# PSUM handed out by single banks, and score pieces issued two by two, in an attention and MLP kernel

## The chip, the core and the metric

The kernel runs on one core of one Trainium2 chip. The metric is the device time of one execution in microseconds (us). Five engines work side by side, each through its own queue in order: TensorE (PE in the profile; its weight loads stand apart as PEld), VectorE (DVE), ScalarE (ACT), GpSimd (POOL) and SyncE (SP, which here only issues transfers). They meet through semaphores: an instruction may wait until another engine's count has reached a number. Matmul results go to PSUM, which has eight banks; a bank holds 512 float32 values per partition.

## The reference

Causal attention over 8 batches, 8 heads, 576 tokens and 64 features, with 16 "beacon" keys and values ahead of the sequence that every token sees; then an MLP with a squared ReLU over the 8 x 576 = 4608 tokens of 512 features:

```
k_all = concat([beacon_k, k]);  v_all = concat([beacon_v, v])
scores = q @ k_all.T / 8;       scores[causal] = -1e9
a = exp(scores - max); a /= sum(a)
x = (a @ v_all) laid out as [4608, 512]
h = x @ w_in                    # [4608, 2048]
out = (max(h, 0) ** 2) @ w_out  # [4608, 512]
```

## The kernel before, in words

**The attention.** The work goes by batch (8) and head pair (4), so 32 pairs. q and k are brought into a transposed form: for batches 0 to 2 on TensorE (line 405, with copies out of PSUM at 280 and 282), later by transposing transfers on SP (line 359). A pair's **scores** are matmuls with 64 rows, the two heads side by side in the two halves of the array (line 506). They come in *pieces*: four for a whole pair, 992, 928, 832 and 576 elements over both heads (batch 0 is split into two phases, with pieces of its own). A piece fills a two-bank tile of PSUM, ScalarE takes its exponential into SBUF (line 520), VectorE masks the diagonal (lines 530 and 534), TensorE multiplies with the values (line 550, with a column of ones that gives the row sums), VectorE normalizes (lines 565 and 566). The result is transposed into `xT`, on TensorE for batches 0 and 1 (line 614), by SP's transfers later (line 597).

**The MLP.** It goes by nine chunks of 512 tokens. For each chunk there are eight *units* (`emit_s1`, line 678): a unit makes two of the sixteen 128-wide slices of the hidden layer, eight matmuls of 512 columns into the two banks of one PSUM tile. One ReLU of 1024 elements empties the tile, on ScalarE (line 694) or VectorE (line 696), and VectorE squares (line 703). The second product (`emit_s2`, line 718) has two PSUM tiles per chunk, each with two token tiles of 128, 32 matmuls in all into each; ScalarE copies each tile out at once, 1024 elements (line 280), but for the last of the kernel, which is copied in two halves, and SP stores it (lines 750 and 752). Chunk 0 has its units in two parts (tokens 0 to 239 and 240 to 511).

**PSUM.** `ps` is four tiles `[128, 2, 512]` in float32, two banks each. Scores, value products, transposes and MLP units all take whole tiles from this one pool.

**The order.** A planner in the kernel's source (`Order.run`) decides it on the host: every operation has an engine (or two to choose from), an assumed duration, a priority, dependencies, and what it takes from a pool and gives back. The planner steps through time, starts on each free engine the ready operation of lowest priority number, and so fixes each engine's order of instructions and the PSUM tile of every operation. `limits` bounds how many tiles a class may hold (scores 2, value products 2, MLP 2, transposes 1). A `gate` holds the scores of a pair back until the MLP has made enough progress. The instructions are then emitted in that order, each engine's queue runs in order on the chip, and the framework puts in the semaphore waits between them from the tiles that they read and write.

Of the kernel before, what the change touches and what calls it, by code (L numbers as in the profile page):

```python
# [10 lines left out]
BF16 = mybir.dt.bfloat16  # L11
# [5 lines left out]
class Op:  # L17
# [4 lines left out]
                 "sync", "insts")  # L22

    def __init__(self, name, engs, dur, emit, prio=0.0, deps=(), take=None, give=None,
                 gate=None, dma=0.0, pe_time=0.0, behind=(), sync=()):
        self.name = name
        self.engs = engs if isinstance(engs, (tuple, list)) else (engs,)
        self.dur = dur
        self.emit = emit
        self.prio = prio  # L30
        self.sync = list(sync)
        self.need = list(deps) + self.sync
        self.users = []
        self.take = take
        self.give = give
        self.gate = gate
        self.held = None
        self.dma = dma
        self.pe_time = pe_time
        self.behind = list(behind)  # L40
        self.followers = []


class Order:
# [3 lines left out]
    LAT = {"PE": 0.2, "ACT": 0.2, "DVE": 0.15, "POOL": 0.25, "SP": 0.1, "-": 0.0}  # L48

    def __init__(self, pools, limits):  # L50
        self.pools = {k: list(v) for k, v in pools.items()}
        self.limits = dict(limits)
        self.inuse = {k: 0 for k in limits}
        self.ops = []
        self.progress = 0.0
# [7 lines left out]
    def run(self):  # L63
# [23 lines left out]
        now = 0.0  # L87
        while events:
            now = events[0][0]
            while events and events[0][0] <= now + 1e-9:  # L90
# [6 lines left out]
                elif kind == "give":  # L97
                    pool, cls, idx = op.give.held
                    self.pools[pool].append(idx)
                    if cls in self.inuse:  # L100
                        self.inuse[cls] -= 1
            again = True
            while again:
                again = False
                for e in engines:
# [3 lines left out]
                    fallback = None  # L109
                    for op in avail[e]:  # L110
                        if any(free[x] <= now + 1e-9 for x in op.engs[:op.engs.index(e)]):
                            continue
                        if op.take:
                            pool, cls = op.take
                            if not self.pools[pool]:
                                continue
                            if cls in self.limits and self.inuse[cls] >= self.limits[cls]:
                                continue
# [20 lines left out]
                    if op.take:  # L139
                        pool, cls = op.take  # L140
                        op.held = (pool, cls, self.pools[pool].pop(0))
                        if cls in self.inuse:
                            self.inuse[cls] += 1
                    dur = op.dur[e] if isinstance(op.dur, dict) else op.dur
                    end = now + dur
# [31 lines left out]
def kernel(  # L177
# [65 lines left out]

    def wait_for(later, first):
# [4 lines left out]
        pools={"ps": range(4), "stg": range(NSTG), "pt": range(NPT)},  # L249
        limits={"strip": 2, "av": 2, "mlp": 2, "tp": 1},  # L250
# [60 lines left out]
    def add_load(b, x, c, prio, behind=[], sync=[]):  # L311
# [10 lines left out]
        def emit_load(e):  # L322
            st = stg[ld.held[2]]
            insts = []
            if lo:
# [6 lines left out]
                 prio=prio, take=("stg", "stg"), dma=1.1 * rows / 128, behind=load_chain[-1:] + behind, sync=sync)  # L332
        load_chain.append(ld)

        def emit_cast(e):
            st = stg[ld.held[2]]
# [40 lines left out]
    def add_strided(b, prio):  # L377
# [17 lines left out]
        for pr in range(HP):  # L395
# [3 lines left out]
            def emit_tp(e, pr=pr, h=h, box=box):  # L399
                pp = ps[box["t"].held[2]].bitcast(BF16)  # L400
                nc.tensor.transpose(pp[:, 1, 0:Nb], bks[b % 2][:, h, :], ident[0:Nb, 0:Nb])
                for half, at, t in ((1, Nb, ks), (0, 0, qs)):
                    for u in range(NS):
# [5 lines left out]
            tp = add(f"tp{b}.{pr}", "PE", 0.8 if b else 1.3, emit_tp, prio=100.0 * (HP * b + pr) - 190,  # L409
                     deps=[bk, loads[pr, "k"], loads[pr, "q"], ident_op] + busy, take=("ps", "tp"))  # L410
            box["t"] = tp

            def emit_k(e, pr=pr, box=box):
                pp = ps[box["t"].held[2]].bitcast(BF16)
# [4 lines left out]
            def emit_q(e, pr=pr, box=box):  # L419
                pp = ps[box["t"].held[2]].bitcast(BF16)  # L420
# [3 lines left out]
            ek = add(f"ek{b}.{pr}", "DVE", 0.9, emit_k, prio=-200.0, deps=[tp])  # L424
            eq = add(f"eq{b}.{pr}", ("DVE", "ACT"), 0.75, emit_q, prio=-199.0, deps=[tp])
# [50 lines left out]
    def add_pair(b, pr):  # L476
# [12 lines left out]
        take_pt = add(f"pt{p}", "-", 0.0, None, prio=100.0 * p, deps=qk_deps, take=("pt", "pt"), gate=gate)  # L489
# [4 lines left out]
    def add_phase(b, pr, p, n, ph, take_pt, qk_deps, gate):  # L494
        base = 100.0 * p + 1000.0 * n
        exps = []
        for i, (mms, off, width) in enumerate(ph.pieces):
            cols = sum(max(96, t1 - t0) for _, t0, t1, _ in mms)
            box = {}

            def emit_qk(e, mms=mms, box=box):
                st = ps[box["qk"].held[2]]
                for c, t0, t1, at in mms:
                    for hj in range(2):
                        hp = slice(64 * hj, 64 * hj + 64)
                        nc.tensor.matmul(  # L506
                            st[:, hj, at:at + t1 - t0],
                            kT[b % 2][hp, pr, 128 * c:128 * c + 128],
                            qT[b % 2][hp, pr, t0:t1],
                            start=True, stop=True,  # L510
                        )

            qk = add(f"qk{p}.{n}.{i}", "PE", 0.05 + cols / 2400.0, emit_qk, prio=base + i,
                     deps=qk_deps + [take_pt], take=("ps", "strip"), gate=gate)
            box["qk"] = qk
            qk_ops[p].append(qk)

            def emit_exp(e, off=off, width=width, box=box):
                st = ps[box["qk"].held[2]]
                nc.scalar.activation(pt[take_pt.held[2]][:, :, off:off + width], st[:, :, 0:width],  # L520
                                     AF.Exp, bias=0.0, scale=scale)

            exps.append(add(f"exp{p}.{n}.{i}", "ACT", 0.18 + 2 * width / 1200.0, emit_exp, prio=base + i,
                            deps=[qk], give=qk))

        def emit_mask(e):
            P = pt[take_pt.held[2]]
# [9 lines left out]
        mask = add(f"mask{p}.{n}", "DVE", 0.15 + 0.14 * ph.diag[3] + (0.25 if ph.last else 0.0), emit_mask,  # L537
# [3 lines left out]
        def emit_av(e):  # L541
            P = pt[take_pt.held[2]]
            a = ps[av.held[2]]
            for hj in range(2):
                h = 2 * pr + hj
                for t in tl:
# [10 lines left out]
        av = add(f"av{p}.{n}", "PE", 0.07 + 0.064 * sum(t + 1 for t in tl), emit_av, prio=base - 150,  # L557
                 deps=[mask] + [cast[b, "v", c] for c in range(tl[-1] + 1)] + av_ops[p], take=("ps", "av"),
# [3 lines left out]
        def emit_norm(e):  # L562
            a = ps[av.held[2]][:, :, 0:nt * (D + 1)].rearrange("p h (t d) -> p h t d", d=D + 1)
# [12 lines left out]
        norm_ops[p, n] = add(f"norm{p}.{n}", "DVE", 0.4 + 0.133 * nt, emit_norm, prio=base - 150, deps=deps, give=av)  # L576
# [27 lines left out]
    def add_xt_pe(b):  # L604
        for k, ph in enumerate(phases(b)):
            for pr in range(HP):
# [3 lines left out]
                def emit_tp(e, pr=pr, box=box, ph=ph):  # L610
                    pp = ps[box["t"].held[2]].bitcast(BF16)
                    for t in ph.tiles:
                        n = t_rows(t)
                        nc.tensor.transpose(pp[:, 0, t_start(t):t_start(t) + n],
# [3 lines left out]
                         deps=[norm_ops[HP * b + pr, k]], take=("ps", "tp"))  # L618
                box["t"] = tp

                def emit_ev(e, pr=pr, box=box, lo=lo, hi=hi):
                    pp = ps[box["t"].held[2]].bitcast(BF16)
                    at = (b * S) % RING
                    copy_on(e, xT[:, pr, at + lo:at + hi], pp[:, 0, lo:hi])

                o = add(f"xte{b}.{k}.{pr}", ("ACT", "DVE"),
                        {"ACT": 0.2 + (hi - lo) / 1200.0, "DVE": 0.12 + (hi - lo) / 960.0}, emit_ev, prio=-110.0,
# [25 lines left out]
    def add_chunk(j):  # L653
# [11 lines left out]
        for f in range(NFT // 2):  # L665
            sqs = []
            for n, (lo_, hi_) in enumerate(parts):
                spans = [(lo_, wrap), (wrap, hi_)] if lo_ < wrap < hi_ else [(lo_, hi_)]
                N = hi_ - lo_
                box = {}  # L670

                def emit_s1(e, f=f, spans=spans, box=box):
                    h = ps[box["s1"].held[2]]
                    for u in range(2):
                        ft = 2 * f + u
                        for lo, hi in spans:
                            for mc in range(NMC):
                                nc.tensor.matmul(h[:, u, lo - spans[0][0]:hi - spans[0][0]],  # L678
# [4 lines left out]
                s1 = add(f"s1.{j}.{f}.{n}", "PE", 1.73 * N / TCH, emit_s1, prio=base + f + 0.5 * n,  # L683
                         deps=feeds_of(lo_, hi_) + [w_ops["in", f // 2]]
                         + [s2_ops[j - 2, u] for u in range(2) if j >= 2],
                         take=("ps", "mlp"), pe_time=1.73 * N / TCH)
                box["s1"] = s1
                s1_ops[lo_, hi_].append(s1)

                def emit_relu(e, f=f, lo=lo_ - t0, hi=hi_ - t0, box=box):  # L690
                    h = ps[box["s1"].held[2]][:, :, 0:hi - lo]
                    dst = G[:, 2 * f:2 * f + 2, lo:hi]
                    if e == "ACT":
                        nc.scalar.activation(dst, h, AF.Relu, bias=0.0, scale=1.0)  # L694
                    else:
                        nc.vector.tensor_scalar(out=dst, in0=h, scalar1=0.0, scalar2=None, op0=ALU.max)  # L696

                rl = add(f"relu{j}.{f}.{n}", ("ACT", "DVE"), {"ACT": 0.2 + N / 600.0, "DVE": 0.15 + N / 480.0},
                         emit_relu, prio=-20.0, deps=[s1], give=s1)
# [5 lines left out]
                sqs.append(add(f"sq{j}.{f}.{n}", "DVE", 0.1 + 0.6 * N / TCH, emit_sq, prio=-10.0, deps=[rl]))  # L705
            sq.append(sqs)
        prevs = {}
        if j == 0:
            order2 = [(u, [(ts, 4 * qd, 4 * qd + 4) for ts in range(2)], [qd]) for qd in range(4) for u in range(2)]
        else:  # L710
            order2 = [(u, [(ts, 8 * half, 8 * half + 8)], [2 * half, 2 * half + 1])
# [122 lines left out]
```

## Time and profile before

| | |
|---|---|
| time, median of 3 runs | 355.47 us (355.32 to 355.49) |
| span of the profiled execution, first to last instruction | 353.2 us |
| matmuls of the MLP's first product, line 678 (records) | 689 |
| matmuls of the MLP's second product, line 718 (records) | 554 |
| score matmuls, line 506 | 400 in 81 uninterrupted runs |
| exponentials, line 520 | 128, 105.3 us of ScalarE |
| ReLUs | 65 on ScalarE (61.8 us), 15 on VectorE (15.8 us) |
| output copies, ScalarE | 19, 18.3 us |

The profile comes from one execution; its own time is its span plus what lies around it, and the median of the runs is 2.3 us above the span. Its views: busy time per engine, also in 40 slices of the span with the clock that TensorE was granted; the chain of work that ended last, followed back from the end; groups of instructions by source line and shape, with count, busy time, mean duration in ns, and the idle time before them with what ended it; the list of waits (engine and line, what it waited for, us in total, times, longest); the timeline. In a row such as `PE L678 MATMUL ps<-xT,w_in 128*128 128x512 bf16 x8` the operation writes `ps` and reads `xT` and `w_in`, on 128 rows and 128 columns of the array, with 512 moving columns, eight times. A matmul's record runs on past the moment at which the next can start, so matmul durations overlap; what counts for the stream is from start to start. Some matmul records are missing.

### The profile page before, as it was taken

Reading aid. Unit: us, or ns where it says so; the run is one execution under the profiler, and the core shown is the slowest. Engines: PE = TensorE matmul, PEld = TensorE weight load, DVE = VectorE, ACT = ScalarE, POOL = GpSimd, SP = SyncE. Lnnn points to the kernel's source line nnn. Section 1 sums busy time; section 2 is a strip of 40 time slices with the busy share of each in tenths; the row PEclk is TensorE's granted clock in tenths of the full one; section 3 lists DMA queues with packets and bytes.
Section 4 is the critical chain, followed back from the end, with each engine's and each line's share of the span. In section 5 each row is a group of like instructions: output and inputs, shape, how many; then the busy total and the mean of one; then the engine's idle time right before and its main releaser. Section 6 shows DMA issues by size and latency. Waiting matters only on the chain.

```text
span 353.2 us, 7173 instructions
## 1 busy us (share of the span) xinstructions
PE 334.7 (95%) x2943; PEld 178.6 (51%) x2980; DVE 148.9 (42%) x287; ACT 193.4 (55%) x233; POOL 85.5 (24%) x132
## 2 busy tenths in 40 slices
PE   3789999999999989999999999999999999999994
PEld 2459665554545444444446874445454444444441
DVE  5576674349714455146622753247132302301300
ACT  2686786287555764665745663676634405505602
POOL 7273721209215504133501651000000000000000
PEclk9999999999999999999999999999999999999999
DMA  7999999965969999699989999440013103003003
GB/s 101 183 160 204 223 206 211 201 169 118 206 116 236 223 221 191 138 224 222 251 137 202 248 213 209 115 118 11 0 61 69 59 0 121 0 0 121 0 0 119
DMA packets 137008, 49.49 MB, mean 140 GB/s; under 512 B 123344, under 2 KB 132048, under 8 KB 136976
## 3 DMA queue, kind: packets, MB, share of 16 engines
q1 hardware_dynamic: 127472, 40.09, 53.4%
q0 software_dynamic: 9504, 8.95, 15.7%
q8 instruction: 23, 0.38, 0.5%
q14 instruction: 9, 0.07, 0.1%
HBM read 37.22 MB, written 9.44 MB: 132 GB/s over the span
## 4 chain that ended last, share of the span: by engine, by line
PE 74%; DMA 12%; SPq 5%; ACT 4%; DVE 2%; issue 2%; POOL 1%; ACTq 0%; DVEq 0%; POOLq 0%
PE ps L678 32%; PE ps L718 27%; PE ps L550 7%; PE ps L506 6%; DMA stg<-in_k_dram 4%; DMA stg<-in_v_dram 4%; SPq L597 3%; ACT pt L520 2%; DMA kT<-qk_area 2%; DMA stg<-in_q_dram 1%; SPq L327 1%; DVE kT L282 1%; DMA qk_area<-in_q_dram 1%; PE ps L405 1%; ACT qT L280 1%
## 5 line engine op out<-in xcount | busy, mean ns | idle before, releaser
L678 PE MATMUL ps<-xT,w_in 128*128 128x512 bf16 (+3 forms) x689 | 131.9, 340 | 1.6 <-ACT qT L280 0.6
L718 PE MATMUL ps<-w_out,g 128*128 128x512 bf16 x554 | 129.5, 380 | 1.4 <-issue 0.5
L520 ACT ACTIVATE pt<-ps 128x832 bf16<-128x832 f32 (+4 forms) x128 | 105.3, 865 | 40.7 <-PE ps L506 40.2
L678 PEld LDWEIGHTS <-w_in 128*128 128x128 bf16 x704 | 66.0, 98 | 57.6 <-issue 6.0
L694 ACT ACTIVATE g<-ps 128x1024 bf16<-128x1024 f32 (+2 forms) x65 | 61.8, 951 | 54.0 <-PE ps L678 53.8
L718 PEld LDWEIGHTS <-g 128*128 128x128 bf16 x576 | 53.0, 98 | 65.7 <-issue 5.8
L703 DVE TENSOR_TENSOR g<-g 128x1024 bf16<-128x1024 bf16 (+2 forms) x80 | 53.0, 664 | 77.5 <-ACT g L694 77.0
L530 DVE TENSOR_TENSOR pt<-pt,tri 128x1024 bf16<-128x1024 bf16 (+1 forms) x36 | 24.8, 692 | 50.1 <-ACT pt L520 48.6
L282 POOL CAST qk_area<-stg 128x512 bf16<-128x512 f32 (+2 forms) x50 | 34.6, 704 | 35.0 <-DMA stg<-in_k_dram 18.7
L282 POOL CAST vb<-stg 128x512 bf16<-128x512 f32 (+1 forms) x38 | 26.0, 695 | 69.6 <-DMA stg<-in_v_dram 59.1
L506 PE MATMUL ps<-qT,kT 64*128 64x80 bf16 (+6 forms) x400 | 39.1, 291 | 1.7 <-DMA kT<-qk_area 1.0
L280 ACT COPY osb<-ps 128x1024 f32<-128x1024 f32 (+1 forms) x19 | 18.3, 969 | 40.6 <-PE ps L718 40.3
L550 PEld LDWEIGHTS <-pt 128*128 128x128 bf16 (+1 forms) x960 | 34.5, 99 | 8.8 <-issue 2.5
L550 PE MATMUL ps<-vb,pt 128*128 128x65 bf16 (+1 forms) x960 | 36.5, 196 | 1.9 <-DVE pt L530 0.9
L566 DVE TENSOR_TENSOR xn<-ps,rcp 128x640 bf16<-128x640 f32 (+2 forms) x36 | 27.0, 750 | 1.7 <-DMA xT<-xn 0.4
L506 PEld LDWEIGHTS <-kT 64*128 64x128 bf16 x400 | 13.7, 97 | 24.2 <-issue 18.8
L565 DVE RECIPROCAL rcp<-ps 128x10 f32<-128x10 f32 (+2 forms) x36 | 7.6, 211 | 38.1 <-PE ps L550 36.2
L696 DVE TENSOR_SCALAR g<-ps 128x1024 bf16<-128x1024 f32 (+2 forms) x15 | 15.8, 1053 | 7.8 <-PE ps L678 7.0
L280 ACT COPY qT<-ps 128x576 bf16<-128x576 bf16 x12 | 7.7, 640 | 16.1 <-DVE kT L282 13.0
L282 DVE COPY kT<-ps 128x16 bf16<-128x16 bf16 (+1 forms) x24 | 9.9, 456 | 9.7 <-PE ps L405 7.5
L405 PE MATMUL ps<-ident,qk_area 96*64 96x96 bf16 x288 | 11.1, 233 | 2.9 <-DMA qk_area<-in_k_dram 1.8
L534 DVE TENSOR_TENSOR pt<-pt,tri 80x160 bf16<-80x160 bf16 x32 | 10.8, 339 | 0.0
(31 smaller groups left out, 57.1 us busy)
## 6 DMA issues: line engine op xcount, KB each, us to landing
out_dram<-osb SPq DMA_DIRECT2D x17, 512.0 KB, 3.5
stg<-in_v_dram SPq DMA_DIRECT2D x21, 256.0 KB, 5.1
stg<-in_q_dram SPq DMA_DIRECT2D x20, 256.0 KB, 4.8
stg<-in_k_dram SPq DMA_DIRECT2D x15, 256.0 KB, 5.1
w_in<-in_moe_w_in_dram POOLq DMA_DIRECT2D x4, 512.0 KB, 8.2
w_out<-in_moe_w_out_dram POOLq DMA_DIRECT2D x4, 512.0 KB, 10.6
stg<-in_v_dram SPq DMA_DIRECT2D x7, 224.0 KB, 4.7
qk_area<-in_k_dram POOLq DMA_DIRECT2D x4, 288.0 KB, 12.4
```

The costliest lines, as they stand in the source:

```text
L280: nc.scalar.copy(dst, src)
L282: eng[e].tensor_copy(dst, src)
L506: nc.tensor.matmul(st[:, hj, at:at + t1 - t0], kT[b % 2][hp, pr, 128 * c:128 * c + 128], qT[b % 2][hp, pr, t0:t1], start=True, stop=True,)
L520: nc.scalar.activation(pt[take_pt.held[2]][:, :, off:off + width], st[:, :, 0:width], AF.Exp, bias=0.0, scale=scale)
L530: nc.vector.tensor_tensor(out=d, in0=d, in1=tri[:, m0:m0 + m, :][:, None].to_broadcast([128, 2, m, 128]), op=ALU.min)
L550: nc.tensor.matmul(a[:, hj, (t - tl[0]) * (D + 1):(t - tl[0] + 1) * (D + 1)], P[0:rr, hj, o:o + 128], vb[b % 2][0:rr, c, h, :], start=(c = ...
L566: nc.vector.tensor_tensor(out=xn[b % 2].rearrange("p t (h d) -> p h t d", d=D)[:, 2 * pr:2 * pr + 2, tl[0]:tl[0] + nt], in0=a[:, :, :, 0:D ...
L678: nc.tensor.matmul(h[:, u, lo - spans[0][0]:hi - spans[0][0]], w_in_sb[:, mc, ft * 128:(ft + 1) * 128], xT[:, mc, lo % RING:lo % RING + hi ...
L694: nc.scalar.activation(dst, h, AF.Relu, bias=0.0, scale=1.0)
L696: nc.vector.tensor_scalar(out=dst, in0=h, scalar1=0.0, scalar2=None, op0=ALU.max)
L703: nc.vector.tensor_tensor(out=d, in0=d, in1=d, op=ALU.mult)
L718: nc.tensor.matmul(o[:, ts, :], G[:, fc, (2 * u + ts) * 128:(2 * u + ts + 1) * 128], w_out_sb[:, fc, :], start=(fc == 0), stop=(fc == NFT ...
```

## The change

1. PSUM is still the same four tiles of two banks, but the pool hands out single banks (0 to 7; banks 2i and 2i+1 are the halves of tile i). A class asks for a list of sizes: `[2]` for a score piece, a value product or a transpose of q and k, `[2, 2]` for two score pieces, `[1]` for an MLP unit, an output tile or a transpose of a result. For a single bank the pool prefers one whose partner is not free, then the lowest number. The limits are doubled, since they now count banks, and the MLP is kept to `floors["mlp"]` banks while an operation that needs several pieces and comes first by priority cannot get them.
2. An MLP unit makes one 128-wide slice in one bank: four matmuls. There are 16 per chunk, each with its own ReLU of 512 elements; the square still covers two slices and waits for both ReLUs.
3. The second product has one bank per token tile of 128, and each is copied out by itself (512 elements). Two copies go into one store, as before; at the end of the kernel each has its own.
4. For batches 1 to 7 two score pieces are one operation: their matmuls are issued one right after the other, into two tiles, and each tile is given back after its own exponential.
5. The planner adds `DRAIN` (0.096) to a TensorE operation whose `mode` (rows, columns, full) differs from that of the one before. Its assumed durations and latencies have new values.

The diff, cut to its core:

```diff
+class Banks:
+    def __init__(self):
+        self.free = set(range(8))
+    def find(self, wants):
+        left = set(self.free)
+        got = []
+        for n in wants:
+            if n == 2:
+                pick = next((b for b in range(0, 8, 2) if b in left and b + 1 in left), None)
+            else:
+                pick = min(left, key=lambda b: (b ^ 1 in left, b), default=None)
+            if pick is None:
+                return None
+            got.append(pick)
+            left -= {pick, pick + 1} if n == 2 else {pick}
+        return got
...
+    DRAIN = 0.096
...
+                    if e == "PE":
+                        dur += self.DRAIN * (mode not in (None, op.mode))
+                        mode = op.mode
...
+    def bank(op, k=0):
+        return ps[op.held[k] // 2][:, op.held[k] % 2, :]
...
-        pools={"ps": range(4), "stg": range(NSTG), "pt": range(NPT)},
-        limits={"strip": 2, "av": 2, "mlp": 2, "tp": 1},
+        pools={"ps": Banks(), "stg": Slots(NSTG), "pt": Slots(NPT)},
+        limits={"strip": 4, "av": 4, "mlp": 4, "tp": 2},
+        floors={"mlp": 2},
...
-        for i, (mms, off, width) in enumerate(ph.pieces):
+        twos = 2 if b >= NSPLIT else 1
+        for i in range(0, len(ph.pieces), twos):
+            group = ph.pieces[i:i + twos]
...
+            qk = add(f"qk{p}.{n}.{i}", "PE", cols / 2400.0, emit_qk, prio=base + i,
+                     deps=qk_deps + [take_pt], take=("ps", "strip", [2] * len(group)), gate=gate, mode="rows")
...
+                rls = []
+                for ft in (2 * f, 2 * f + 1):
...
-                    h = ps[box["s1"].held[2]]
-                    for u in range(2):
-                        ft = 2 * f + u
+                        h = bank(box["s1"])
                         for lo, hi in spans:
                             for mc in range(NMC):
...
-                        nc.scalar.activation(dst, h, AF.Relu, bias=0.0, scale=1.0)
+                            nc.scalar.activation(dst, h, AF.Relu, bias=0.0, scale=1.0)
...
-                sqs.append(add(f"sq{j}.{f}.{n}", "DVE", 0.1 + 0.6 * N / TCH, emit_sq, prio=-10.0, deps=[rl]))
+                sqs.append(add(f"sq{j}.{f}.{n}", "DVE", 0.05 + N / 870.0, emit_sq, prio=-10.0, deps=rls))
...
+        step = 4 if j == 0 else 8
+        order2 = ([(ts, f0) for f0 in range(0, NFT, step) for ts in range(4)] if j == 0 else
+                  [(ts, f0) for ts in range(4) for f0 in range(0, NFT, step)])
...
+                evs.append(add(f"ev{j}.{ts}", "ACT", act(d_model), emit_ev, prio=-15.0,
+                               deps=[s2_ops[j, ts]] + st_ops.get(2 * j + u - 2, []), give=s2_first[j, ts]))
```

261 lines of the change are left out of this document (142 added, 119 removed).

## The prediction, on record before the result

> **What bounds the kernel now.** I read the page first, for engine shares and the chain; then the list of waits, for what TensorE waits on; then the timeline, where two kinds of matmul meet; then the groups by shape, for ScalarE and VectorE prices.
>
> ```profile
> span 353.2 us, 7173 instructions
> ## 1 busy us (share of the span) xinstructions
> PE 334.7 (95%) x2943; PEld 178.6 (51%) x2980; DVE 148.9 (42%) x287; ACT 193.4 (55%) x233; POOL 85.5 (24%) x132
> ...
> PEclk9999999999999999999999999999999999999999
> ...
> PE 74%; DMA 12%; SPq 5%; ACT 4%; DVE 2%; issue 2%; POOL 1%; ACTq 0%; DVEq 0%; POOLq 0%
> ...
> L520 ACT ACTIVATE pt<-ps 128x832 bf16<-128x832 f32 (+4 forms) x128 | 105.3, 865 | 40.7 <-PE ps L506 40.2
> ```
>
> ```profile
> PE ps L401 <- DVE bks L373: 4.2, 1, 4.2
> PE ps L405 <- DMA qk_area<-in_k_dram: 1.8, 3, 1.2
> ...
> PE ps L506 <- DMA kT<-qk_area: 1.0, 1, 1.0
> ...
> PE ps L678 <- ACT qT L280: 0.6, 1, 0.6
> ...
> PE ps L550 <- ACT pt L520: 0.2, 1, 0.2
> PE ps L506 <- ACT pt L520: 0.2, 1, 0.2
> ```
>
> TensorE is busy for 95% of the span and carries 74% of the chain. Its waits are short and early (4.2 and 1.8 us before the first scores); for ScalarE it waits 1.0 us in all (0.6, 0.2, 0.2). So ScalarE, at 55%, is hidden, and every new wait of TensorE lengthens the kernel by its own size.
>
> **Prices.** All from these rows:
>
> ```profile
> 334.30 13.70 PEld L718 LDWEIGHTS <-g 128*128 128x128 bf16 x64
> ```
> ```profile
> 151.61 1.90 PE L678 MATMUL ps<-xT,w_in 128*128 128x512 bf16 x8
> ...
> 153.44 0.58 PE L506 MATMUL ps<-qT,kT 64*128 64x496 bf16 x4
> 153.54 1.02 ACT L694 ACTIVATE g<-ps 128x1024 bf16<-128x1024 f32 x1 [1.12 <-PE ps L678]
> ...
> 153.95 1.90 PE L718 MATMUL ps<-w_out,g 128*128 128x512 bf16 x8
> ```
> ```profile
> 44.27 0.64 ACT L280 COPY qT<-ps 128x576 bf16<-128x576 bf16 x1 [0.87 <-DVE kT L282]
> ...
> 44.96 0.62 PE L678 MATMUL ps<-xT,w_in 128*128 128x272 bf16 x4 [0.65 <-ACT qT L280]
> ```
> ```profile
> L694 ACT ACTIVATE g<-ps 128x1024 bf16<-128x1024 f32 x54 | 55.3, 1024 | 50.5 <-PE ps L678 50.4
> ...
> L280 ACT COPY osb<-ps 128x1024 f32<-128x1024 f32 x17 | 17.2, 1014 | 39.9 <-PE ps L718 39.6
> ...
> L694 ACT ACTIVATE g<-ps 128x480 bf16<-128x480 f32 x7 | 4.0, 571 | 2.7 <-PE ps L678 2.7
> ...
> L694 ACT ACTIVATE g<-ps 128x544 bf16<-128x544 f32 x4 | 2.5, 630 | 0.7 <-PE ps L678 0.7
> ...
> L280 ACT COPY osb<-ps 128x512 f32<-128x512 f32 x2 | 1.1, 589 | 0.7 <-PE ps L718 0.7
> ```
>
> - Matmul slot: 64 weight loads, one per 512-column matmul, take 13.70 us; less the last load's 0.10 that is 63 slots, 0.216 us each. A new unit of four is 0.863 us.
> - Drain: the eight matmuls from 151.61 need 1.726 us, yet the scores start 1.83 later: 0.10. The scores (496 and 464 columns, two heads side by side) need 960/512 x 0.216 = 0.405, and line 718 starts 0.51 later: 0.10 again. So each change between 64-row scores and full-row work costs 0.10 us.
> - TensorE to ScalarE: the unit's last slot ends at 151.61 + 1.73 = 153.34; the ReLU starts at 153.54: 0.20.
> - ScalarE to TensorE: the copy ends at 44.27 + 0.64 = 44.91; the waiting matmul starts at 44.96: 0.05.
> - A ReLU of 512 elements: between 571 ns (480) and 630 ns (544), so 0.60. A copy of 512 is 0.589.
>
> A **full trip**, unit done, ReLU, next unit, is 0.20 + 0.60 + 0.05 = 0.85 us in which TensorE stands, if nothing else is queued on it.
>
> **The change part by part.**
>
> *Scores two by two.* I counted runs of equal row form in both kernels' TensorE instruction order. Score runs fall from 81 to 66 and form changes from 172 to 147. 25 x 0.10 = **-2.4 us**, on the path. The planner's new durations and its drain term issue no instruction; they act through the order alone.
>
> *One-bank units.* 80 ReLUs (65 on ScalarE, 15 on VectorE) become 160 (128 and 32); 19 output copies become 36. ScalarE pays 2 x 0.60 - 1.024 = 0.18 on each of some 54 full-width ReLUs, and 2 x 0.589 - 1.014 = 0.16 on each of 17 copies: 12 us more on an engine with 160 us free. By itself nothing; it matters only where TensorE waits for it.
>
> *What TensorE now waits for.* The allocator prefers a bank whose partner is taken, so with nothing else open the MLP alternates between the two banks of one tile. The tiles are still four of two banks, and in the changed kernel's built instruction list the waits go by tile. From the last chunk:
>
> ```
> matmuls 2857-2860, unit into bank 6    waits for ScalarE's 290th
> ScalarE's 291st, ReLU from bank 7      waits for matmul 2860
> matmuls 2861-2864, unit into bank 7    waits for ScalarE's 291st
> ScalarE's 292nd, ReLU from bank 6      waits for matmul 2864
> ```
>
> The ReLU of bank 7 needs matmul 2856 alone, but it is issued after the unit into bank 6 of the same tile, and waits for that too. That unit's own follower waits for the ReLU. So neither runs beside the other: unit, trip, unit, trip. Before, the rotation went over whole tiles and no such pair existed.
>
> From the last batch's scores on (the end of chunk 6, all of 7 and 8) I count the TensorE waits whose ScalarE instruction itself waits for the matmul just before: 47 at units, 12 at the output matmuls. No work lies between, so each pays the full trip: 59 x 0.85 = **+50.2 us**. Behind each waiting matmul the whole TensorE queue stands; ScalarE, VectorE (the squares) and SP (the stores) wait for that.
>
> *Waits with some cover, chunks 0 to 6.* 47 more waits have scores or value matmuls between, too short for the trip. The typical one: two score pieces (576 + 416 columns, 0.39 with one drain 0.49) between the units of a tile's two banks, 0.85 - 0.49 = 0.36. Per wait I took the trip (0.20, the ScalarE or VectorE work from that matmul on, 0.05), less the matmuls between, less what an earlier wait in the same stretch already gave. Units behind a ScalarE ReLU, 18 waits: 7.4 us. Behind an output copy, 11: 5.1. Where the one bank's ReLU is on VectorE and the other's, on ScalarE, waits for it, 9: 6.6. Others, 9: 2.7. Together **+21.8 us**. VectorE's price for 512 is 0.69, from
>
> ```profile
> L696 DVE TENSOR_SCALAR g<-ps 128x480 bf16<-128x480 f32 x1 | 0.7, 658 | 0.6 <-ACT pt L520 0.6
> ...
> L696 DVE TENSOR_SCALAR g<-ps 128x544 bf16<-128x544 f32 x4 | 2.9, 720 | 2.0 <-PE ps L678 2.0
> ```
>
> This term is the least sure. Below, it is 10 if exponentials and masks give more cover than counted; a gain is excluded, since the chip holds each wait. Above, a ReLU can find ScalarE in an exponential of 0.865: if every second one does, 23 x 0.865 = 20 more.
>
> *Opening.* The same count gives 6 us in the first 20 us of TensorE work against 4 before: **+2**. Between 0 (loads end those waits) and 5.
>
> *Queues.* SP and POOL issue the same transfers; on SP some transposes of batches 2 to 7 move past loads, and POOL's order is as before. TensorE's 1.0 us wait for a transposed k falls into slack when the stream is 20 us longer: nothing counted.
>
> *End.* The last two copies are 128x512 before and after, and both wait for the last matmul of all (2980), again by tile: nothing.
>
> **Sum**: 353.2 - 2.4 + 50.2 + 21.8 + 2 = 424.8 us of span; less 1 for waits of this kind that the rotation of before already had (1.0 above). What lies around the span is 355.5 - 353.2 = 2.3. **426 us**, against the median of 355.47.
>
> **Rivals.**
>
> *The clock falls.* Here TensorE would be busy 0.86 of every 1.71 us through the units of chunks 6 to 8. The trace has one such broken stream, the opening:
>
> ```profile
> 20.58 0.51 PE L550 MATMUL ps<-vb,pt 128*128 128x65 bf16 x6 [0.88 <-DVE pt L530]
> ...
> 22.60 1.52 PE L550 MATMUL ps<-vb,pt 128*128 128x65 bf16 x24
> ...
> 24.77 0.89 PE L550 MATMUL ps<-vb,pt 128*128 128x65 bf16 x24
> ```
>
> The same 24 matmuls take 1.52 us and two microseconds later 0.89, although the row of the granted clock reads 9 throughout: half speed until a dense stretch has passed, so a broken stream did not earn full speed. Whether one that has it loses it, nothing of before shows. If the 47 units ran at half speed: 47 x 0.86 = 40 more, 466 us. The Trainium skill, "TensorE: Matmul & The Clock Gate", section "A second HAM failure mode: psum-queue depth-cycling", says that cycling through banks with short idles between groups makes the clock swing; its Part 1 wants a whole idle window of about 3.4 us. The trace, with no gap over 1 us once at full speed, bears out neither.
>
> *ScalarE becomes the bound between scores.* The queue of exponentials delays the ReLUs as priced above: 446 us. For it: the page's 55% are an average, and 128 exponentials share ScalarE with the ReLUs there. Against it: each TensorE stall gives ScalarE time to catch up.
>
> *Not slower.* If a ReLU had only its own bank's unit to wait for, its 0.85 would lie beside the other bank's 0.863 and no serial trip arise; the point is trip below unit. Then the drains are left, and the first of the last two copies goes beside matmuls: 353.2 - 2.4 - 0.6 + 2.3 = 352.5 us. The Trainium skill, "PSUM — Partial Sum Buffer", section "PSUM bank collisions raise a hardware error", asks for guarding by bank and has two engines on different banks run clean: by that page the chip allows it. Against it stand the wait values in the list.
>
> *The covered waits are covered.* With nothing for the 47 and the opening: 402 us.
>
> **How the numbers follow.** Forecast (408 to 440) 0.70, ScalarE-bound 0.13, clock 0.09, waits covered 0.05, not slower 0.03. The range takes in the forecast and the ScalarE case: 408 to 448. 0.2% (0.7 us) is about what a measurement of this kernel can tell from no change. Faster and the same come from the case "not slower" alone, 352.5 being 3 us under: 0.02 and 0.01. Slower: 0.97.
>
> **What would show it.** In the last 130 us: TensorE in groups of four, starts 1.71 us apart, with 0.7 us idle between, ended by ScalarE (0.85, less the 0.17 that a matmul runs past its slot: 1.90 less 8 x 0.216); TensorE's waits for ScalarE 40 us or more in the list, from 1.0; the chain's ScalarE share from 4% to over 10%; no ReLU of 128x1024; 512-column matmuls 0.216 apart inside every group (0.43 would be the clock). Form changes stay 0.10 each. Units 0.86 apart without idle would make it wrong; so would 59 trips of 0.85 with a time outside the range, and then the covered waits are the step that failed.

## The result and the profile after

| | before | after |
|---|---|---|
| time, median | 355.48 us (355.32 to 355.91, 4 runs) | 429.32 us (429.10 to 432.06, 4 runs) |
| ratio | | 1.2096 (95% interval 1.2074 to 1.2119) |
| span of the profiled execution | 353.2 us | 430.4 us |
| form changes of TensorE, counted in the instruction list | 172 | 147 |

The kernel became 73.8 us slower; 426.0 was forecast, with a range of 408 to 448. The profiled execution of after is the slowest of its four (432.06 us; TensorE's clock dropped for a short while in it, which cost about 3 us, see the last section); the other three have spans of 427.4, 427.4 and 427.8 us.

The page of after, its span, busy times, granted clock and the chain by engine:

```profile
span 430.4 us, 7314 instructions
## 1 busy us (share of the span) xinstructions
PE 351.1 (82%) x2980; PEld 182.4 (42%) x2980; DVE 149.9 (35%) x306; ACT 199.9 (46%) x311; POOL 84.4 (20%) x132
...
PEclk9999799999999999999999999999999999999999
...
PE 71%; ACT 17%; DVE 4%; issue 4%; ACTq 0%; DVEq 0%
```

TensorE has the same 2980 matmuls and falls from 95% to 82% of the span. ScalarE does 6.5 us more work than before (199.9 for 193.4) and is nevertheless busy for a smaller share, 46% after 55%. So it is not the engine that is full; but its share of the chain went from 4% to 17%. An engine that is rarely busy and often on the chain is one that others wait for, not one that lacks time.

TensorE's waits in after (engine and line, releaser: us in total, times, longest):

```profile
PE ps L755 <- ACT g L772: 39.6, 66, 0.9
PE ps L792 <- ACT osb L355: 7.8, 15, 0.8
PE ps L792 <- ACT g L772: 4.9, 7, 0.8
PE ps L476 <- ACT qT L355: 4.7, 5, 1.7
PE ps L755 <- ACT osb L355: 4.5, 7, 0.8
PE ps L584 <- ACT g L772: 4.5, 9, 0.6
```

Before, all waits for ScalarE came to 1.0 us. Here the six rows make 66.0, and 39.6 of them are MLP units (line 755) behind a ReLU (line 772). The longest of these is 0.9 us. Many equal short waits, and no long one, are the mark of a handover that is paid each time.

The timeline of after in chunk 8, four columns of start, duration, engine with operation, and idle time before it:

```profile
395.06 0.60 ACT L772 ACTIVATE g<-ps 128x512 bf16<-128x512 f32 x1 [1.11 <-PE ps L755]
395.71 1.02 PE L755 MATMUL ps<-xT,w_in 128*128 128x512 bf16 x4 [0.69 <-ACT g L772]
...
396.77 0.60 ACT L772 ACTIVATE g<-ps 128x512 bf16<-128x512 f32 x1 [1.11 <-PE ps L755]
...
397.42 1.02 PE L755 MATMUL ps<-xT,w_in 128*128 128x512 bf16 x4 [0.69 <-ACT g L772]
```

Unit at 395.71, ReLU at 396.77, unit at 397.42: 1.71 us from unit to unit. The ReLU of 396.77 ends at 397.37, and the unit starts 0.05 later. Both engines work by turns, and each waits for the other. The groups by shape give the prices:

```profile
L772 ACT ACTIVATE g<-ps 128x512 bf16<-128x512 f32 x105 | 60.9, 596 | 95.5 <-PE ps L755 64.4 <-DVE g L774 22.7 <-PE ps L792 7.2
...
L355 ACT COPY osb<-ps 128x512 f32<-128x512 f32 x36 | 20.8, 586 | 78.2 <-PE ps L792 66.5 <-PE ps L755 7.8 <-issue 3.8
...
L774 DVE TENSOR_SCALAR g<-ps 128x512 bf16<-128x512 f32 x23 | 15.9, 692 | 41.7 <-PE ps L755 39.5 <-PE ps L792 2.1
```

A ReLU of 512 takes 596 ns on ScalarE and 692 on VectorE, a copy 586: the prediction had taken 0.60 and 0.69 from the neighbouring shapes, and 0.589 from the two copies of this shape in the kernel before.

### The profile page after: what moved, and what is told of

Its sections match the earlier page's. It is cut to its first block, busy times and chain, and to the rows that moved or that the text cites. A ratio compares the mean times of both kernels' runs of the same rounds, so it can differ in the third digit from the quotient of the medians.

```text
span 430.4 us, 7314 instructions
## 1 busy us (share of the span) xinstructions
PE 351.1 (82%) x2980; PEld 182.4 (42%) x2980; DVE 149.9 (35%) x306; ACT 199.9 (46%) x311; POOL 84.4 (20%) x132
## 4 chain that ended last, share of the span: by engine, by line
PE 71%; ACT 17%; DVE 4%; issue 4%; ACTq 0%; DVEq 0%
PE ps L755 30%; PE ps L792 29%; ACT g L772 12%; PE ps L627 6%; PE ps L584 5%; ACT osb L355 3%; DVE g L774 2%; PE ps L480 1%; DVE g L781 1%; ACT pt L597 1%; DVE kT L357 1%; ACT qT L355 1%; PE ps L691 1%; ACT xT L355 0%; PE ps L476 0%
## 5 line engine op out<-in xcount | busy, mean ns | idle before, releaser
L755 PE MATMUL ps<-xT,w_in 128*128 128x512 bf16 (+3 forms) x704 | 143.3, 343 | 45.1 <-ACT g L772 39.6
L792 PE MATMUL ps<-w_out,g 128*128 128x512 bf16 x576 | 132.0, 379 | 13.4 <-ACT osb L355 7.8
L772 ACT ACTIVATE g<-ps 128x512 bf16<-128x512 f32 (+2 forms) x128 | 68.7, 559 | 103.2 <-PE ps L755 71.4
L755 PEld LDWEIGHTS <-w_in 128*128 128x128 bf16 x704 | 67.6, 98 | 110.7 <-issue 64.2
L792 PEld LDWEIGHTS <-g 128*128 128x128 bf16 x576 | 54.7, 97 | 82.0 <-issue 21.4
L355 ACT COPY osb<-ps 128x512 f32<-128x512 f32 x36 | 20.8, 586 | 78.2 <-PE ps L792 66.5
L584 PE MATMUL ps<-qT,kT 64*128 64x80 bf16 (+6 forms) x400 | 37.0, 292 | 6.3 <-ACT g L772 4.5
L607 DVE TENSOR_TENSOR pt<-pt,tri 128x1024 bf16<-128x1024 bf16 (+1 forms) x36 | 22.9, 639 | 43.4 <-ACT pt L597 41.9
L774 DVE TENSOR_SCALAR g<-ps 128x512 bf16<-128x512 f32 (+2 forms) x32 | 19.6, 614 | 47.8 <-PE ps L755 44.4
L480 PEld LDWEIGHTS <-qk_area 96*64 96x64 bf16 x288 | 8.9, 132 | 6.4 <-DMA qk_area<-in_k_dram 2.5
```

The costliest lines, as they stand in the source:

```text
L355: nc.scalar.copy(dst, src)
L480: nc.tensor.transpose(pp[64 * hj:64 * hj + 64, half, at + u * NP:at + (u + 1) * NP], t[b % 2][:, 2 * pr + hj, u, :], ident[0:NP, 0:NP])
L584: nc.tensor.matmul(st[:, hj, at:at + t1 - t0], kT[b % 2][hp, pr, 128 * c:128 * c + 128], qT[b % 2][hp, pr, t0:t1], start=True, stop=True,)
L755: nc.tensor.matmul(h[:, lo - spans[0][0]:hi - spans[0][0]], w_in_sb[:, mc, ft * 128:(ft + 1) * 128], xT[:, mc, lo % RING:lo % RING + hi - lo],
L792: nc.tensor.matmul(o, G[:, fc, ts * 128:(ts + 1) * 128], w_out_sb[:, fc, :], start=(fc == 0), stop=(fc == NFT - 1))
```

## The experiments

**The theory** is that of the prediction: the waits between engines follow the PSUM tile and not the bank, and since the allocator puts consecutive units into the two banks of one tile, unit and ReLU run one after the other. **Rivals**: the chip itself does not let TensorE write one bank while ScalarE reads its neighbour; more and smaller ScalarE instructions are what costs; the order with paired scores is what costs; TensorE's clock fell. Except where two kernels are compared, the ratio is to the kernel before on the same chip (medians of before 355.38 for the first four, 355.09 for the next four, 355.42 for the last two). It is not the plain quotient of the two medians and can differ a little from it.

| kernel | time, us | ratio to before (95%) |
|---|---|---|
| after | 429.32 | 1.2096 (1.2074 to 1.2119) |
| eight_tiles | 350.08 (349.05 to 350.40) | 0.9837 (0.982 to 0.9855) |
| split_only | 430.06 (430.01 to 431.58) | 1.2101 (1.2079 to 1.2124) |
| other_tile | 356.02 (354.99 to 359.48) | 1.0028 (1.0002 to 1.0053) |
| scores_only | 356.26 (355.21 to 357.61) | 1.0024 (1.0007 to 1.0041) |
| last_chunk | 412.05 (411.31 to 414.03) | 1.1613 (1.1571 to 1.1655) |
| relu_vector | 432.46 (431.67 to 434.55) | 1.2178 (1.2139 to 1.2217) |
| three_two | 354.09 (353.11 to 355.47) | 0.9969 (0.9954 to 0.9983) |
| units_only | 434.69 (434.30 to 435.05) | 1.2231 (1.2207 to 1.2256) |
| eight_nopair | 353.47 (352.67 to 353.99) | 0.9941 (0.9925 to 0.9957) |
| eight_again | 349.74 (349.45 to 350.10) | 0.9843 (0.9826 to 0.9859) |

### eight_tiles: the same banks and the same planned order, but each bank is a tile

```diff
-    ps = [psum.tile([128, 2, 512], FP32, name=f"ps{i}") for i in range(4)]
+    ps = [psum.tile([128, 512], FP32, name=f"ps{i}") for i in range(8)]
...
-        return ps[op.held[k] // 2][:, op.held[k] % 2, :]
+        return ps[op.held[k]]
...
-                    nc.scalar.activation(pt[take_pt.held[0]][:, :, off:off + width],
-                                         pair(box["qk"], k)[:, :, 0:width], AF.Exp, bias=0.0, scale=scale)
+                    for h in range(2):
+                        nc.scalar.activation(pt[take_pt.held[0]][:, h, off:off + width],
+                                             half(box["qk"], h, k)[:, 0:width], AF.Exp, bias=0.0, scale=scale)
```

An exponential or a normalization over both banks of a piece can't span two tiles, so it becomes two instructions, one for each head. The 2980 matmuls come in the same order as in after, and each writes the same bank.

> PSUM is declared as eight tiles of one bank in place of four of two; what needs two banks (exponentials, normalizations) is issued as two instructions, one per head. Planner, order of the operations and bank numbers are those of the changed kernel. Theory (waits go by tile, so the two banks of a tile never work at once): no wait is left between neighbouring banks; the 59 full trips (50 us) and the 47 covered ones (22 us) go, the first of the last two copies goes beside matmuls (0.6), and 128 more exponentials at 0.18 us of fixed cost (23 us) lie on ScalarE, which has the room: 351 to 357 us. In the last 130 us units start 0.86 us apart. Rival (single-bank units and copies cost by themselves, or ScalarE reading one bank slows TensorE writing its neighbour): the units are the same and the banks are the same, so 425 us or more. Rival (the new order of the scores is what costs): order unchanged, 425 us or more.

350.08 us, 0.9 under the expected range: the 74 us are gone, and the kernel is 1.4% to 1.8% faster than before. The timeline of eight_tiles in chunk 8:

```profile
317.80 4.51 PE L757 MATMUL ps<-xT,w_in 128*128 128x512 bf16 x20
...
319.11 0.60 ACT L774 ACTIVATE g<-ps 128x512 bf16<-128x512 f32 x1 [0.29 <-PE ps L757]
...
319.97 0.60 ACT L774 ACTIVATE g<-ps 128x512 bf16<-128x512 f32 x1 [0.27 <-PE ps L757]
...
320.83 0.60 ACT L774 ACTIVATE g<-ps 128x512 bf16<-128x512 f32 x1 [0.27 <-PE ps L757]
```

Twenty matmuls without a gap, 0.216 apart, with a ReLU every 0.86 us beside them: the ReLU of one bank runs while the next unit fills another. The Trainium skill, "PSUM — Partial Sum Buffer", section "PSUM bank collisions raise a hardware error", has two engines on different banks run clean; this trace agrees, with TensorE writing for the whole of each 0.60 us. So the chip does not force the turns. ScalarE does more here than in after:

```profile
PE 336.2 (96%) x2980; PEld 177.9 (51%) x2980; DVE 159.3 (46%) x378; ACT 209.7 (60%) x439; POOL 86.8 (25%) x132
...
PE 92%; DMA 2%; SPq 2%; DVE 1%; ACT 1%; issue 0%; POOL 0%; ACTq 0%; POOLq 0%
```

209.7 us against 199.9 of after, 439 instructions against 311, and 1% of the chain. No cost of the smaller ScalarE instructions is to be seen here, where nothing waits for them.

### split_only: its control, the divided instructions on the four two-bank tiles

```diff
-        return ps[op.held[k] // 2]
+        return ps[op.held[k] // 2][:, h, :]
...
-                    nc.scalar.activation(pt[take_pt.held[0]][:, :, off:off + width],
+                    for h in range(2):
+                        nc.scalar.activation(pt[take_pt.held[0]][:, h, off:off + width],
```

> The control for the run with eight tiles: exponentials and normalizations split by head in the same way, but PSUM stays four tiles of two banks. Theory: all 59 full trips and the 47 covered waits stay; the split adds ScalarE work between the scores, of which TensorE sees 0 to 6 us: 429 to 436 us. Rival (it is the split that makes the run with eight tiles what it is): near that run's time.

430.06 us, as slow as after. Here too the matmuls keep their order and their banks. Dividing the exponentials gives nothing; the size of the tile is the whole difference between 430 and 350.

### other_tile: one line of the allocator

```diff
-                pick = min(left, key=lambda b: (b ^ 1 in left, b), default=None)
+                pick = min(left, key=lambda b: (b ^ 1 not in left, b), default=None)
```

> One line is changed: a single bank is chosen whose partner is free, in place of one whose partner is taken. Tiles and waits stay as the framework makes them. Theory: neighbouring units land in different tiles, so a ReLU of 0.60 + 0.25 us lies beside the next unit's 0.86; my count of waits leaves none of full length and 3.6 us of covered ones; form changes stay at 147: 353.2 - 2.4 + 3.6 + 2 (opening) - 1 + 2.3 = 357 us, 352 to 360. Rival (single-bank units cost by themselves): 425 us or more, the units are the same. Rival (the order of the scores costs): 425 or more, if the scores keep their order, since their form changes are equal in number.

356.02 us. The tiles, the unit size, the ReLUs and the paired scores are those of after; only the preference is turned round, so that a single bank is taken from a tile that is wholly free. The planner's order shifts somewhat with that; the form changes stay at 147. Of the 66 us of TensorE's waits for ScalarE in after, the list of other_tile keeps these as the largest:

```profile
PE ps L476 <- ACT qT L355: 3.9, 4, 1.7
PE ps L755 <- ACT g L772: 1.9, 6, 0.7
PE ps L584 <- ACT pt L597: 1.0, 2, 0.8
```

### scores_only: paired scores, and the MLP in whole tiles as before

```diff
-                             take=("ps", "mlp", [1]), pe_time=us)
+                         take=("ps", "mlp", [2]), pe_time=1.73 * N / TCH)
...
-                        h = bank(box["s1"])[:, 0:hi - lo]
+                    h = pair(box["s1"])[:, :, 0:hi - lo]
```

> One part of the change alone: score pieces two by two, single-bank pool and new planner durations stay, but MLP units, ReLUs and output tiles are those of before, in whole tiles. Theory: no two classes share a tile, no trips; form changes 145 against 172 of before, 27 x 0.10 = 2.7 us less; against that 4.2 us of covered waits counted in the lists (before has 1.0), some of them where a pair of scores holds two tiles and a unit must wait for the third: 355.5 - 2.7 + 3.2 = 356 us, 352 to 359. Rival (paired scores are what costs): well above 400 us.

356.26 us. The paired scores don't cost the 74 us. They bring nothing here either, although this kernel has 145 form changes, 27 fewer than before. Its largest waits for ScalarE:

```profile
PE ps L476 <- ACT qT L355: 3.5, 3, 1.7
PE ps L755 <- ACT g L771: 3.3, 5, 0.7
PE ps L584 <- ACT pt L597: 1.1, 1, 1.1
```

With two smaller rows (0.6 and 0.5) TensorE waits 9.0 us for ScalarE, where before had 1.0. Against these 8.0 us stand the 27 x 0.10 = 2.7 us of form changes and 3.3 us less of waits for transfers (0.7 after 4.0). That would leave the kernel 2.0 us slower, and 0.9 were measured (356.26 against 355.38), so the balance is closed only roughly. The first row stands in other_tile too (3.9): the first transpose of a head pair, which waits until ScalarE has copied the q of an earlier pair out of PSUM. Why the planner's new order runs into this was not tried.

### last_chunk: the other choice of bank in chunk 8 alone

```diff
+class Far(list):
+    pass
...
-                pick = min(left, key=lambda b: (b ^ 1 in left, b), default=None)
+                far = isinstance(wants, Far)
+                pick = min(left, key=lambda b: ((b ^ 1 in left) != far, b), default=None)
...
-                             take=("ps", "mlp", [1]), pe_time=us)
+                             take=("ps", "mlp", Far([1]) if j == 8 else [1]), pe_time=us)
```

> The changed kernel with one exception: in chunk 8, and only there, a single bank is chosen whose partner is free. Theory (each full trip costs 0.85 us by itself): 20 of the 59 full trips are those of chunk 8, the other 39 and all covered waits stay: 429.3 - 20 x 0.85 = 412.3 us, 411 to 414; in the last 27 us units 0.86 us apart, in chunk 7 still 1.71. Rival (the time is lost elsewhere and only shows at these waits, so that it comes back at others): less than half of the 17 us.

412.05 us: 20 of the 59 trips are gone, for 429.32 - 412.05 = 17.3 us, 0.86 each (0.85 was the price). The two were measured separately, and the medians of before beside them differ by 0.4 us (355.48 and 355.09). In the list of waits the rows of units and output matmuls behind ReLUs and copies made 95 waits in after (66 + 7 + 15 + 7). Here they make 74, 21 fewer:

```profile
PE ps L760 <- ACT g L777: 30.2, 51, 0.9
PE ps L797 <- ACT osb L360: 6.4, 13, 0.8
...
PE ps L797 <- ACT g L777: 3.5, 5, 0.8
PE ps L760 <- ACT osb L360: 3.1, 5, 0.8
```

This is the test that the price is per trip: a stretch without trips returns their sum and no more.

### relu_vector: the ReLUs of the last two chunks on VectorE

```diff
-                        if e == "ACT":
+                        if e == "ACT" and j < 7:
```

> The changed kernel, order and banks untouched, but the ReLUs of chunks 7 and 8 are issued on VectorE. Theory: 32 trips get longer by the difference of the two engines' ReLUs of 512, 0.69 against 0.60 us: 32 x 0.09 = 2.9 us more, 432 us (431 to 433), with units of chunks 7 and 8 1.80 us apart in place of 1.71. Rival (TensorE's stop is a fixed price of switching banks and the ReLU is not in it): units stay 1.71 apart, 429.3 us.

432.46 us. The engine changes and the turns stay, longer by the longer ReLU:

```profile
405.23 1.02 PE L755 MATMUL ps<-xT,w_in 128*128 128x512 bf16 x4 [0.78 <-DVE g L774]
406.29 0.69 DVE L774 TENSOR_SCALAR g<-ps 128x512 bf16<-128x512 f32 x1 [1.11 <-PE ps L755]
...
407.04 1.02 PE L755 MATMUL ps<-xT,w_in 128*128 128x512 bf16 x4 [0.78 <-DVE g L774]
```

1.81 us from unit to unit in place of 1.71, for a ReLU of 0.69 in place of 0.60. In these chunks VectorE has little else to do (in after 16.6 us of the last 135). So it is not ScalarE's load, and not ScalarE at all; whoever reads the tile holds it.

### three_two: three tiles of two banks and two of one

```diff
-    ps = [psum.tile([128, 2, 512], FP32, name=f"ps{i}") for i in range(4)]
+    ps = [psum.tile([128, 2, 512], FP32, name=f"ps{i}") for i in range(3)]
+    one = [psum.tile([128, 512], FP32, name=f"one{i}") for i in range(2)]
...
-                pick = min(left, key=lambda b: (b ^ 1 in left, b), default=None)
+                pick = next((b for b in (6, 7) if b in left), None)
```

Units, output tiles and result transposes have the two small tiles to themselves; chunk 0's second product goes token tile by token tile, so that two banks are enough.

> Three tiles of two banks for scores, values and transposes of q and k, two tiles of one bank for the MLP and the transposes of results; exponentials are whole again; chunk 0's second product goes token tile by token tile. Theory: a tile is either a pair or a single bank, so no two operations ever share one; 146 form changes and 1 us of covered waits in the lists: 350 to 356 us, at or a little above the run with eight tiles, as the MLP has two banks only and a ReLU behind an exponential (0.87) can stop it. Rival (single-bank units cost by themselves): above 420 us.

354.09 us, ratio 0.9969 (0.9954 to 0.9983). Two banks are enough for the units to run without trips, with the exponentials left whole: the unit slot of 0.863 us just covers the trip of 0.85. The kernel lies 4.0 us above eight_tiles; its list has 5.2 us in which transposes wait for ScalarE's copies of q, a row that eight_tiles does not have. Whether that is the cause was not tried.

### units_only: the change without the pairing

```diff
-        twos = 2 if b >= NSPLIT else 1
+        twos = 1
```

> The changed kernel without the pairing of score pieces: each piece is an operation of its own again; units, pool and tiles stay as changed. Theory: the 59 full trips of chunks 6 to 8 stay; form changes 152 against 147 (0.5 us more); fewer scores lie between neighbouring units, and my count of the other waits is 6 us higher: 429 to 438 us, 436 likeliest. Rival (the pairing of the scores is what costs): back near 355 us.

434.69 us, 5.4 slower than with the pairing. The one-bank units bring the whole slowdown without the pairing, and the pairing earns part of it back.

### eight_nopair and eight_again: what the pairing is worth without the trips

The edit of eight_nopair is that of units_only, on top of eight_tiles; eight_again is the kernel of eight_tiles once more, on the same chip.

> Eight one-bank tiles, but the score pieces issued one at a time. Form changes 152 against 147 with the pairing, so 5 x 0.10 = 0.5 us more than eight_tiles if a form change is all that the pairing saves: 350.6 us beside 350.1. Rival: the pairing carries the whole of the 25 fewer form changes' gain or more, as the prediction's wording had it: 2.4 us, 352.5 or above. A second rival: single pieces let ScalarE's exponential begin sooner and the kernel is faster than eight_tiles, 349.6 or below.

> The kernel of eight_tiles once more, so that the one without pairing has its partner on the same chip: 350.1 (349 to 351).

353.47 and 349.74 us: the pairing is worth 3.7 us, not the 0.5 of its five form changes. The first rival holds in size, but not in its cause: without the pairing 152 form changes are left, so 20 of the 25 fewer are not the pairing's. Of the 3.9 us between the two spans (351.6 and 347.7), one wait in the list of eight_nopair makes 1.4:

```profile
PE ps L584 <- DVE g L783: 1.4, 1, 1.4
```

In its timeline TensorE stands from 130.04 to 131.44, with all score matmuls behind it. The five form changes make 0.5. The full clock comes 0.9 us later (26.1 for 25.2 us after the span's start), which at half speed is up to 0.45. Some 1.5 us stay open: a different order moves many small things, and no single one of them was tried.

## Why the prediction was right

Its mechanism is shown, by the pair eight_tiles and split_only from one side and by the one-line other_tile from the other. Step by step:

- **59 full trips, +50.2.** I set every matmul's start against its slot of 0.216 us per 512 columns. From span 294 us on 59 matmuls start late, 47 at units and 12 at the second product, which is the forecast count, by 50.4 us in all. Each trip behind a ReLU took 0.846 to 0.849, each behind an output copy 0.880 to 0.892. The 0.04 more behind a copy is where the term was small: eleven of these, 11 x 0.04 = 0.4.
- **Partly covered waits, +21.8.** As eight_tiles has the same matmuls in the same order, every start of after can be set against its counterpart there. Between span 39.5 and 294 us TensorE loses 23.8 us behind ReLUs and output copies: 5.2 in 11 waits behind copies, for which the prediction had 11 waits and 5.1, and 18.6 in 43 waits behind ReLUs. One of those behind an output copy, in the timeline of after:

```profile
246.12 0.58 PE L584 MATMUL ps<-qT,kT 64*128 64x496 bf16 x4
246.63 3.63 PE L792 MATMUL ps<-w_out,g 128*128 128x512 bf16 x16
250.19 0.48 PE L584 MATMUL ps<-qT,kT 64*128 64x336 bf16 x8
250.93 0.38 PE L792 MATMUL ps<-w_out,g 128*128 128x512 bf16 x1 [0.26 <-ACT osb L355]
```

  After the line before it, the matmul of 250.93 comes 0.33 us later than its counterpart in eight_tiles.
- **What the prediction left out.** Two ReLUs in a row on ScalarE, from the two banks of a tile, and TensorE behind the second:

```profile
111.78 0.48 PE L584 MATMUL ps<-qT,kT 64*128 64x336 bf16 x8
111.88 1.08 ACT L772 ACTIVATE g<-ps 128x512 bf16<-128x512 f32 x2 [1.06 <-PE ps L755]
...
113.02 1.67 PE L792 MATMUL ps<-w_out,g 128*128 128x512 bf16 x7 [0.76 <-ACT g L772]
```

  Five such places (at 113, 181, 191, 222 and 227 us) cost 2.8 of the 23.8 us. The prediction priced the series of a VectorE and a ScalarE ReLU, but not that of two on ScalarE. Without them its term of 21.8 measures 21.0.
- **Opening, +2, and the sum.** Up to span 39.5 us after falls 2.5 us behind eight_tiles. The prediction added 50.2 + 21.8 + 2 - 1 = 73.0 us of waits; measured are 50.4 + 23.8 + 2.5 = 76.7, or 3.7 more, of which 2.8 are the five places. The forecast span was 423.8, and the three executions without the drop of the clock have 427.4 to 427.8: 3.6 more at least. The two agree closely, but one is counted from before and the other from eight_tiles, so small errors may cover each other.
- **Drains, -2.4.** The size is right: in the fence above the scores at 246.12 need 0.405 and the next line starts 0.51 later. The cause was named wrongly. The prediction put all 25 fewer form changes under "scores two by two"; units_only has 152, so 20 of them come with the planner's drain term, its new durations and the smaller units, and only 5 with the pairing. And as a saving it only counts where no wait takes its place: scores_only and other_tile have 145 and 147 form changes and are not faster than before.
- **ScalarE's 12 us more: nothing.** The nothing is right, by eight_tiles, where ScalarE does still more. Added one by one, ScalarE's instructions do take 11.4 us more than before, but its busy time grows by 6.5 only: instructions in a row overlap, as the two ReLUs of 596 ns above, which take 1.08 us together.
- **End: nothing.** Right: in after both last copies wait for the last matmul,

```profile
426.05 1.07 ACT L355 COPY osb<-ps 128x512 f32<-128x512 f32 x2 [5.47 <-PE ps L792]
```

  while in eight_tiles the first of them runs 1.7 us earlier, beside matmuls:

```profile
343.32 0.58 ACT L355 COPY osb<-ps 128x512 f32<-128x512 f32 x1 [4.58 <-PE ps L794]
...
345.06 0.59 ACT L355 COPY osb<-ps 128x512 f32<-128x512 f32 x1 [1.15 <-PE ps L794]
```

- **The rival "not slower", 352.5,** was right about its condition. Where a ReLU waits only for its own bank, the time is 350.1. It lay 2.4 us too high; of the 5.3 us that eight_tiles gains on before, the form changes (2.4) and the end (0.6) are named, and the rest was not taken apart.
- **"ScalarE becomes the bound"** asked for 20 us more of waits between the scores, 41.8 in place of 21.8; there are 23.8, and split_only, which gives ScalarE 8.0 us more work (207.9 for 199.9), is only 0.7 us slower than after. relu_vector does not bear on it, since the last two chunks have no scores. **"The waits are covered"** fell with the 23.8 us. **"The clock falls"** fell for the MLP's stream, which it was about: the granted clock is full through all 59 trips.

## What to carry to other kernels

Handing out halves of a buffer gains nothing as long as the waits are placed by the whole buffer: look in the built instruction list at what a reader of one half waits for, before trusting that two halves work side by side. If there are such halves, an allocator should give consecutive work to different buffers, and one line of preference was worth 73 us here. Count serial handovers by their number times one measured trip: no engine is then full and no instruction is longer, so the loss shows only as many short idle times of TensorE.

## What the runs showed of the hardware that was not expected

TensorE's granted clock fell in the middle of the profiled execution of after. The stretches of 3.4 us around it (us, busy time of each engine, granted clock, DMA share, GB/s), with one of the tail as the last row:

```profile
42.20:45.60 3.40, 3.24 (x46) 2.19 (x45) 2.34 (x5) 1.52 (x4) 2.62 (x5) 1.00 1.24 205
45.60:49.00 3.40, 1.88 (x38) 1.45 (x38) 2.22 (x6) 2.85 (x4) 1.91 (x3) 1.00 1.25 207
49.00:52.40 3.40, 2.91 (x33) 1.91 (x32) 1.63 (x4) 2.32 (x5) 0.00 (x0) 0.50 1.24 207
52.40:55.80 3.40, 3.40 (x25) 1.91 (x24) 1.18 (x3) 2.25 (x4) 0.00 (x0) 0.50 1.31 202
...
400.00:403.40 3.40, 2.03 (x9) 0.77 (x8) 0.69 (x1) 1.19 (x2) 0.00 (x0) 1.00 0.02 5
```

After a stretch in which TensorE was busy for 1.88 of 3.40 us the clock is 0.50 for two stretches, 6.8 us, and the span is 430.4 in place of 427.4: 3 us. Set against eight_tiles matmul by matmul, after loses 2.8 us there beside its waits behind ReLUs. The Trainium skill, "TensorE: Matmul & The Clock Gate", section "Part 1: The HAM clock gate", has the clock go down after an idle window of about 3.4 us. Here the longest idle time at full clock before the fall is 1.06 us, so the trace does not bear out that the window must be idle. Nor is it the busy share alone: the tail has nearly the same, 2.03 of 3.40, for 27 us at a stretch in the units of each of the last three chunks, and keeps the full clock. The Trainium skill, in the section "A second HAM failure mode: psum-queue depth-cycling" of the same page, would have the tail swing, with its short idles between groups in alternating banks; it does not. What differs is the work: 0.87 of the 1.88 us before the fall are transposes with 16 or 96 rows and 0.48 are score matmuls with 64 rows, while the tail has only matmuls of 128 x 128. The profiles of split_only and units_only show such a drop too, from 49.8 and 47.6 us and for 3.4 us each. In all three it comes 23.9 us after the clock rose to full (at 25.1, 25.9 and 23.8 us). The profiles of other_tile, last_chunk, relu_vector and eight_tiles show none. But the drop is not tied to the kernel: three of after's four executions have a mean granted clock of 0.998 or more, while one execution of other_tile (359.48 us) has 0.989 and one each of last_chunk (414.03 us) and relu_vector (434.55 us) 0.990, each 2.0 to 3.5 us above its kernel's median. Whether the kind of matmul decides, or where the stretch falls in time, was not tried and stays open.
